# Attention scores on Trainium2: three 32-partition passes recast as one 64-partition and one 32-partition pass, with two buffers of stacked queries

## The chip, the cores and the metric

The kernel runs on one core of one Trainium2 chip. The metric is device time in microseconds (us): 2056.73 us, the median of 3 runs (2056.43 to 2056.93).

## What is computed

Two rounds of the same two layers run on x, 2048 rows of 448 floats, with the same weights in both rounds:

```python
def _A_ref(x, wq, wk, wv, wo):          # S=2048, D=448, H=16 heads, Dh=28
    q = (x @ wq).reshape(B, S, H, Dh).transpose(0, 2, 1, 3)
    k = x @ wk                          # one key and one value head for all 16
    v = x @ wv
    p = softmax(einsum("bhqd,bkd->bhqk", q, k) * (Dh ** -0.5))
    o = einsum("bhqk,bkd->bhqd", p, v)
    return o.transpose(0, 2, 1, 3).reshape(B, S, H * Dh) @ wo

def _B_ref(x, w_gate, w_up, w_down):    # F=1792
    return (silu(x @ w_gate) * (x @ w_up)) @ w_down

x = x + _A_ref(layernorm(x), ...); x = x + _B_ref(layernorm(x), ...)   # twice
```

## The kernel before, in words

**Number parts.** TensorE (PE) multiplies in a rounded 32-bit format (fp32r). Nearly all operands are therefore kept as a high part (the rounded value) and a low part (what is left), made by `split` (L131 to L133): one GpSimd (POOL) copy and one POOL subtraction. A product of two such operands is taken as three: high by high, low by high, high by low.

**Stages.** For each of the two layers: projections of queries, keys and values (`Attention.project`, `q`), then the scores, the softmax and its product with the values (`Attention.scores`), then the feed-forward layer (`FeedForward`). All engines run the program in the written order (a manual schedule).

**A group and a step.** The 2048 queries are cut into 4 chunks of 512 columns (`c`), the 16 heads into 4 sets of 4 heads (`g`). A group `i` is one pair (c, g): 16 groups in each layer. A step `n` of a group (`step`, L553) treats one tile of 128 keys (`kt`, 16 of them) against 4 heads by 512 queries, so that there are 256 steps in a layer and 512 in the program. Head `j` of the group has its 28 numbers, and 4 more rows for the bound that is subtracted ahead of the exponential, on partitions 32j to 32j+31 of the stacked queries `qts[i % 3]`. Plane 0 of that tile is the high part and plane 1 the low part. `keys[kt // 4]` repeats the same keys on all four blocks of 32 partitions, again with a high and a low plane.

**What PE does in a step.** L558 to L564 issue three passes of four matmuls; each matmul uses the 32 rows of the array of its own head, and the four of a pass use four different row groups. Heads 0 to 2 accumulate in one of two PSUM tiles of three banks (`three`), head 3 in a single bank (`one`). ScalarE (ACT) then takes the exponential of `one` (L567) and of `three` (L568). After the scores of step n, PE does `pv` (L598) of step n - 2: the exponentials as moving operand, with the tile of values as 32 weight columns, so that four heads write four blocks of 32 output partitions. That product is in full f32 and takes two instructions a head in the trace. On PE the order is: scores n, pv n - 2, scores n + 1, pv n - 1, and so on. At step 10 of groups 4, 8 and 12 the output product of the chunk before (`outproj`, L545) comes between the two.

**What feeds it.** `stack` (L371) loads the four heads of group i + 2 from DRAM (`qd`) into `qraw` with four DMAs at step 4 of group i; `parts` (L378) splits them on POOL at step 7; `rows` (L382) puts the bound's rows into partitions 28 to 31 of each block with one DMA at step 9, all DMAs on the queue of SyncE (SP). The first three groups are prepared in the projection stage, where `key_load` and `key_split` (L351, L355) also make the keys, one chunk after another. In the same stage POOL computes `rstd` (L217, L218) of the layer norm, which VectorE (DVE) needs for the normalised rows `xn` (L225), which PE transposes (L242).

`post` (L606) finishes a group: DVE copies the sums, four DMAs bring the denominators, and at step 3 of the next group `rest` sends their reciprocals through DRAM, multiplies and splits on POOL. `weights(fc)` for the feed-forward layer is called at step 8 of groups 11 to 13.

The second run of `forward` with `full=True`, under an If in the outer function, is a fallback that the shown runs do not enter; it shares the functions of the change.

Of the kernel before, what the change touches and what calls it, by code (L numbers as in the profile page):

```python
# [8 lines left out]
F32 = mybir.dt.float32  # L9
F32R = mybir.dt.float32r  # L10
# [5 lines left out]
P = 128  # L16
S = 2048
D = 448
# [8 lines left out]
FG = 2  # L27
SCALE = DH ** -0.5

LEAD = 4  # L30
LIMIT = 2.0**40
TURN = (3, 2, 0, 1)

# [20 lines left out]
def forward(  # L54
# [241 lines left out]

    GR = [(c, g) for c in range(NC) for g in range(NG)]

    class Attention:


        def __init__(self, layer):
            self.layer = layer
            self.X, self.norms, self.qd = {}, {}, {}
            self.done = 0
            self.order = [(c, m) for c in range(NC) for m in TURN]
            self.seen = 0
            self.steps, self.places = [], []
            self.lent, self.plan = None, {}
            self.hi, self.rowsof, self.kt, self.when = {}, {}, {}, {}  # L310
# [12 lines left out]
            for i in range(len(GR) if full else 0):  # L323
                fs, place = self.max_steps(i)
                if i == 1:
                    fs[KC] = lambda f=fs[KC]: (f(), self.places[0]())
                self.steps += fs
                self.places.append(place)

# [40 lines left out]

        def stack(self, i):  # L371

            c, g = GR[i]
            for j in range(4):
                r = 112 * g + DH * j
                nc.sync.dma_start(qraw[32 * j : 32 * j + DH, :], self.qd[c][r : r + DH, :])

        def parts(self, i):  # L378
            q = qts[i % 3]
            split(q[:, 0, :], q[:, 1, :], qraw)  # L380

        def rows(self, i):  # L382

            c, g = GR[i]
            src = self.rowsof[c][32 * g : 32 * g + 32, :].rearrange("n (j w) -> j n w", w=32)
            dst = qts[i % 3][28:125:32, :, :].rearrange("j z (b w) -> j (z b) w", w=32)
            nc.sync.dma_start(dst.bitcast(F32), src)

        def maxima(self, c, cands=ALL):

# [18 lines left out]
        def fetch(self, ms):  # L409

            r = wpool.tile([P, 2, 512], F32R, tag="wgl", name="wrq", bufs=FG + 1).bitcast(F32)
            two = wpool.tile([P, 2, 512], F32R, tag="wgh", name="q2", bufs=FG + 1)
            for z, m in enumerate(ms):
                nc.sync.dma_start(r[0:112, z, :], self.qd[0][112 * m : 112 * m + 112, :])
                self.hi[m] = two[0:112, z, :]
            nc.gpsimd.tensor_copy(two[0:112], r[0:112])

        def max_steps(self, i):

            got = {}  # L420
            q = qts[i % 3]

            def one(j, qt, kc):
                if not got:
                    got["mx"] = pers.tile([P, 16, KC], F32, name="mx", bufs=2)
                n = 4 * j + qt
                pm = self.mbank()[1]
                js, qs = slice(32 * j, 32 * j + 32), slice(P * qt, P * qt + P)
                for n_, (z, k) in enumerate(((0, 0), (1, 0), (0, 1))):
                    nc.tensor.matmul(  # L430
                        pm, q[js, z, qs], keys[kc][js, k, :], start=(n_ == 0), stop=(n_ == 2), tile_position=(32 * j, 0)
                    )
                nc.vector.tensor_reduce(got["mx"][:, n, kc : kc + 1], pm, AX.X, ALU.max)

            def fin():
                got["ng"] = pers.tile([P, 16], F32, name="ng", bufs=2)
                nc.vector.tensor_reduce(got["ng"], got["mx"], AX.X, ALU.max, negate=True)

            def place(pn=None):

                if pn is None:
                    pn = self.mbank()[1]
                nc.tensor.transpose(pn[0:16, 0:P], got["ng"], ident)
                nh = pers.tile([16, P], F32R, name="nh", bufs=2)
# [3 lines left out]
                for z, n_ in enumerate((nh, nl)):  # L448
                    dma(q[28:125:32, z, :].rearrange("j (t w) -> j t w", w=P), n_)
# [27 lines left out]
        def q(self, c, m):  # L477
# [6 lines left out]
                self.maxima(self.seen // 4 - 1)  # L484
            live.remove(held)
            if c not in self.qd:
                self.qd[c] = dram.tile([D, 512], F32, name=f"qd{self.layer}_{c}")
# [7 lines left out]
            nc.sync.dma_start(self.qd[c][112 * m : 112 * m + 112, :], raw[0:112, :])  # L495
# [12 lines left out]
        def finish(self):  # L508

            if self.layer:  # L510
                nc.scalar.activation(warm, halfn[:, 0:1], AF.Exp)
                if not full:
                    self.fetch((3, 2))
                    self.fetch((0, 1))
            while self.seen < len(self.order):
                self.project()
            if not full:
                self.maxima(NC - 1, (6,))
            for n in sorted(self.when):
                for f in self.when[n]:  # L520
                    f()
            self.advance(len(self.steps), NM + KC * LEAD)

        def scores(self, ff):
            next(switch)
            with tc.tile_pool(name=f"at{self.layer}", bufs=1) as wp:
                woh = wp.tile([P, NG, D], F32R, name="woh")
                wol = wp.tile([P, NG, D], F32R, name="wol")
# [24 lines left out]
                def step(n):  # L553

                    i, kt = divmod(n, NT)
                    three, one = threes[n % 2], banks[7]
                    q, k, ks = qts[i % 3], keys[kt // 4], slice(P * (kt % 4), P * (kt % 4) + P)
                    for z, (kp, part) in enumerate(((0, 0), (1, 0), (0, 1))):  # L558
                        for j in range(4):
                            js = slice(32 * j, 32 * j + 32)  # L560
                            nc.tensor.matmul(  # L561
                                three[:, j, :] if j < 3 else one, k[js, kp, ks], q[js, part, :],
                                start=(z == 0), stop=(z == 2), tile_position=(32 * j, 0),
                            )  # L564
                    pt = wp.tile([P, 3, 512], F32, name="pt", bufs=3)
                    pt1 = wp.tile([P, 512], F32, name="pt1", bufs=2 if full else 3)
# [4 lines left out]
                def between_steps(n):  # L571
# [2 lines left out]
                    free, one = threes[(n + 1) % 2], banks[7]  # L574
                    if full:
                        self.lent = free[:, 0, :]
                        self.advance(KC)
# [321 lines left out]
    at.turned(0)  # L899
    nc.gpsimd.memset(vsb, 0.0)  # L900
    nc.gpsimd.memset(vsb[:, :, DH : DH + 1], 1.0)
    nc.gpsimd.memset(qraw, 0.0)
    if mask is not None:
        nc.gpsimd.memset(mask, 0.0)
        nc.gpsimd.memset(mask[:, 0:16:5, :], 1.0)
# [47 lines left out]
```

## Time and profile before

| | |
|---|---|
| median of 3 runs | 2056.73 us |
| the profiled execution's own time | 2054.69 us |
| its span | 2053.0 us |
| PE, PE weight loads (PEld) | 2014.4 us, 1274.7 us busy |
| ACT | 1312.2 us busy |
| POOL, DVE | 535.4 us, 461.2 us busy |
| projections of layer 0 | until about 72 us |
| scores and softmax of layer 0 | about 72 to 597 us |
| feed-forward of layer 0, then the projections of layer 1 | about 597 to 1086 us |
| scores and softmax of layer 1 | about 1086 to 1609 us |
| granted TensorE clock, mean | 0.995 |

A line of a timeline gives the start in us from the start of the span, the duration in us, the engine, the line of the kernel, the operation, output and inputs with their shapes, and a count where equal neighbours are merged. A matmul's duration includes its latency, and neighbours overlap, so the distance from start to start says what it costs in a row of matmuls. "32\*128" is the shape of the array tile that is used: 32 rows (contraction) by 128 columns. In brackets stands the idle time of the engine ahead of the instruction and what is inferred to have ended it.

### The profile page before, as it was taken

The numbers are of one execution on the slowest core, as the hardware profiler recorded it, in microseconds if no ns is written. First come the engines' busy times: TensorE is split into PE (matmuls) and PEld (weight loads), VectorE is DVE, ScalarE is ACT, GpSimd is POOL, SyncE is SP. The second block draws the span as 40 slices with busy tenths as digits, with TensorE's granted clock in tenths as the row PEclk, the third lists the DMA queues.
The fourth block names the chain that finished last, engine by engine and source line by source line (L and its number), as shares of the span: only waits on it lengthen the run. The fifth ranks groups of instructions, "written<-read, shape, count | busy, mean of one in ns | idle before, by whom it ended". The sixth has DMA issues, their size and how long they took to land.

```text
span 2053.0 us, 43566 instructions
## 1 busy us (share of the span) xinstructions
PE 2014.4 (98%) x18577; PEld 1274.7 (62%) x18577; DVE 461.2 (22%) x892; ACT 1312.2 (64%) x2152; POOL 535.4 (26%) x599
## 2 busy tenths in 40 slices
PE   7999999999999999999999999999999999999997
PEld 6433434334358999999874334343343689988887
DVE  7200101001105232322451001010011242232322
ACT  4699798997964333333348998979979533333332
POOL 4213121021311333333341222101122123233320
PEclk9999999999999999999999999999999999999999
DMA  5101000011100111100031110000110000111101
GB/s 158 52 22 28 21 12 22 12 36 27 32 12 19 31 31 30 31 23 19 21 93 34 30 30 12 22 12 22 27 50 8 29 16 16 30 31 31 30 1 74
DMA packets 76516, 63.47 MB, mean 31 GB/s; under 512 B 22904, under 2 KB 63224, under 8 KB 76312
## 3 DMA queue, kind: packets, MB, share of 16 engines
q1 hardware_dynamic: 76040, 60.56, 10.4%
q8 instruction: 147, 2.41, 0.5%
q14 instruction: 57, 0.47, 0.1%
q10 hardware_dynamic: 272, 0.03, 0.0%
HBM read 47.72 MB, written 12.32 MB: 29 GB/s over the span
## 4 chain that ended last, share of the span: by engine, by line
PE 48%; ACT 46%; issue 1%; DVE 1%; DMA 0%; POOL 0%; POOLq 0%; ACTq 0%; DVEq 0%
PE bank L288 38%; ACT pt L568 31%; ACT pt L567 15%; PE bank L268 3%; PE three L545 2%; PE bank L545 2%; PE bank L242 1%; PE bank L598 1%; PE three L561 0%; PE bank L561 0%; DVE xres L732 0%; DVE sg L818 0%; DVE h L822 0%; DVE xn L225 0%; DVE xl L249 0%
## 5 line engine op out<-in xcount | busy, mean ns | idle before, releaser
L568 ACT ACTIVATE pt<-three 128x1536 f32<-128x1536 f32 x512 | 741.1, 1447 | 0.0
L598 PE MATMUL bank<-pt,vsb 128*32 128x512 f32 x4096 | 547.0, 607 | 0.6 <-ACT pt L568 0.6
L561 PEld LDWEIGHTS three<-qstack,keys 32*128 32x128 f32 x4608 | 253.6, 184 | 447.6 <-ACT pt L567 394.1
L561 PE MATMUL three<-qstack,keys 32*128 32x512 f32 x4608 | 500.8, 427 | 0.2 <-ACT pt L568 0.2
L561 PE MATMUL bank<-qstack,keys 32*128 32x512 f32 x1536 | 494.8, 427 | 4.1 <-ACT pt L567 4.1
L288 PE MATMUL bank<-xh,wgh 64*128 64x512 f32 x1728 | 452.3, 390 | 0.4
L288 PE MATMUL bank<-xh,wgl 64*128 64x512 f32 x1404 | 371.4, 390 | 0.0
L567 ACT ACTIVATE pt<-bank 128x512 f32<-128x512 f32 x512 | 305.9, 598 | 77.2 <-PE bank L561 70.7
L288 PE MATMUL bank<-xl,wgh 64*128 64x512 f32 x1296 | 338.6, 390 | 0.0
L288 PE MATMUL bank<-wdh,h 64*128 64x448 f32 x1792 | 334.2, 364 | 1.4 <-ACT h L819 0.8
L288 PEld LDWEIGHTS bank<-xh,wgh 64*128 64x128 f32 x1728 | 268.1, 184 | 17.6 <-DVE xl L249 1.5
L736 POOL TENSOR_TENSOR xres<-stage,xres 128x448 f32<-128x448 f32 x108 | 127.3, 1199 | 499.6 <-ACT stage L735 499.6
L288 PEld LDWEIGHTS bank<-wdh,h 64*128 64x128 f32 x1792 | 247.2, 184 | 15.4 <-issue 2.7
L632 POOL TENSOR_TENSOR o<-o 128x512 f32<-128x512 f32 x32 | 41.0, 1282 | 825.4 <-DMA o<-rd 748.7
L561 PEld LDWEIGHTS bank<-qstack,keys 32*128 32x128 f32 x1536 | 244.9, 184 | 5.8 <-ACT pt L567 5.5
L295 ACT COPY seen<-bank 128x1 f32<-128x1 f32 x664 | 81.9, 163 | 247.9 <-PE bank L288 245.2
L288 PEld LDWEIGHTS bank<-xh,wgl 64*128 64x128 f32 x1404 | 220.6, 184 | 12.5
L288 PE MATMUL bank<-wdl,h 64*128 64x448 f32 x896 | 220.7, 367 | 0.0
L817 ACT ACTIVATE sg<-bank 128x512 f32<-128x512 f32 x112 | 67.3, 601 | 220.1 <-PE bank L288 215.0
L288 PEld LDWEIGHTS bank<-xl,wgh 64*128 64x128 f32 x1296 | 200.3, 184 | 9.3
L598 PEld LDWEIGHTS bank<-pt,vsb 128*32 128x32 f32 x4096 | 80.9, 108 | 191.0 <-issue 176.2
L818 DVE TENSOR_TENSOR sg<-bank,sg 128x512 f32<-128x512 f32 x112 | 77.5, 692 | 501.1 <-ACT sg L817 492.1
(113 smaller groups left out, 1724.8 us busy)
## 6 DMA issues: line engine op xcount, KB each, us to landing
o<-rd SPq DMA_DIRECT2D x32, 256.0 KB
qd<-stage SPq DMA_DIRECT2D x32, 224.0 KB
qraw<-qd SPq DMA_DIRECT2D x128, 56.0 KB
wdr<-in_B_w_down_dram SPq DMA_DIRECT2D x28, 224.0 KB
wr<-in_B_w_gate_dram SPq DMA_DIRECT2D x28, 192.0 KB
wr<-in_B_w_up_dram SPq DMA_DIRECT2D x28, 192.0 KB
out_dram<-xres SPq DMA_DIRECT2D x16, 224.0 KB
xres<-in_A_x_dram SPq DMA_DIRECT2D x3, 896.0 KB
```

The lines of the kernel that those rows point to most:

```text
L268: nc.tensor.matmul(po, a, b, start=(i == 0), stop=(i == len(seq) - 1))
L288: nc.tensor.matmul(po, a, b, start=start, stop=stop, skip_group_check=True)
L295: nc.scalar.copy(seen[:, i : i + 1], po[:, 0:1])
L545: nc.tensor.matmul(po[:, 0:D], a[:, g, ts_], b[:, g, :], start=(g + z == 0), stop=(g == NG - 1 and z == 2))
L561: nc.tensor.matmul(three[:, j, :] if j < 3 else one, k[js, kp, ks], q[js, part, :], start=(z == 0), stop=(z == 2), tile_position=(32 * j, 0),)
L567: nc.scalar.activation(pt1, one, AF.Exp, scale=SCALE)
L568: nc.scalar.activation(pt, three, AF.Exp, scale=SCALE)
L598: nc.tensor.matmul(accs[i][32 * j : 32 * j + 32, :], vsb[:, kt, :], pts[n][j], start=(kt == 0), stop=(kt == NT - 1), skip_group_check=True,)
L632: nc.gpsimd.tensor_tensor(rb, oraw, rb, ALU.mult)
L736: nc.gpsimd.tensor_tensor(r, s, r, ALU.add)
L817: nc.scalar.activation(sg, pg[0], AF.Silu)
L818: nc.vector.tensor_tensor(sg, pg[1], sg, ALU.mult)
```

## The change

The three products of a head are regrouped. On the blocks of 64 partitions 0 to 63 and 64 to 127, plane 0 of the keys now holds the high part of the keys in the lower 32 partitions and their low part in the upper 32; plane 1 holds the high part everywhere. The stacked queries have three planes: planes 0 and 1 hold the high part of heads 0 and 1, and of heads 2 and 3, each head twice in a block of 64 partitions; plane 2 holds the low part of all four heads on 32 partitions each, as before. A step then does four matmuls of 64 rows (heads 0 and 1 beside each other, then heads 2 and 3), and four of 32 rows.

`parts` makes the high part of the doubled tile with one POOL copy of 1024 elements a partition, and the low part from `qraw` with a `split`; `key_split` gets two more POOL copies of 32 partitions. `stack` issues five DMAs and loads 32 rows a head instead of 28, each of four heads twice; `rows` issues three. `qd` gets 128 rows a group instead of 112. There are two buffers of stacked queries instead of three: group i + 1's `parts` are now at step 2 of group i and its `rows` at step 5, and `stack` of group i + 2 at step 9. Only two groups are prepared in the projection stage. The doubled tile lives in a buffer of the feed-forward weights, whose calls move to groups 12 to 14.

```diff
+    qts = [pers.tile([P, 3, 512], F32R, name=f"qstack{n}") for n in range(2)]
-    qts = [pers.tile([P, 2, 512], F32R, name=f"qstack{n}") for n in range(3)]
...
+    def passes(j):
+
+        r = 64 * (j % 2)
+        return (0, slice(r, r + 64), j // 2), (1, slice(32 * j, 32 * j + 32), 2)
...
-            for i in range(3):
+            for i in range(2):
                 self.at(4 + 3 * i, lambda i=i: self.stack(i))
                 self.at(6 + 3 * i, lambda i=i: self.parts(i))
...
         def key_split(self, c):
-            split(keys[c][:, 0, :], keys[c][:, 1, :], self.rep)
+            both, high = keys[c][:, 0, :], keys[c][:, 1, :]
+            split(high, both, self.rep)
+            for r in (0, 64):
+                nc.gpsimd.tensor_copy(both[r : r + 32, :], high[r : r + 32, :])
...
         def stack(self, i):
             c, g = GR[i]
+            src = self.qd[c][P * g : P * g + P, :]
+            if self.twice is None or not self.scoring:
+                self.twice = wpool.tile([P, 2, 512], F32R, tag="wgl", name="qr2", bufs=FG + 1).bitcast(F32)
             for j in range(4):
-                r = 112 * g + DH * j
-                nc.sync.dma_start(qraw[32 * j : 32 * j + DH, :], self.qd[c][r : r + DH, :])
+                head = src[DH * j : DH * j + 32, :][None].to_broadcast([2, 32, 512])
+                nc.sync.dma_start(self.twice[64 * (j % 2) : 64 * (j % 2) + 64, j // 2, :], head)
+            heads = bass.AP(tensor=src.tensor, offset=src.offset, ap=[[DH * 512, 4], [512, 32], [1, 512]])
+            nc.sync.dma_start(qraw, heads)
 
         def parts(self, i):
-            q = qts[i % 3]
-            split(q[:, 0, :], q[:, 1, :], qraw)
+            q = qts[i % 2]
+            nc.gpsimd.tensor_scalar(q[:, 0:2, :], self.twice, 1.0, 0.0, ALU.mult, ALU.add)
+            split(q[:, 2, :], q[:, 2, :], qraw)
...
         def rows(self, i):
...
+            for rs, js, dst in (
+                (slice(0, 16), slice(0, 64), q[28:93:64, 0, :]),
+                (slice(0, 16), slice(64, 128), q[28:93:64, 1, :]),
+                (slice(16, 32), slice(0, 128), q[28:125:32, 2, :]),
+            ):
+                rows = src[rs, js].rearrange("n (j w) -> j n w", w=32)
+                nc.sync.dma_start(dst.bitcast(F32).rearrange("j (n w) -> j n w", w=32), rows)
...
-                    for z, (kp, part) in enumerate(((0, 0), (1, 0), (0, 1))):
+                    for n_ in range(2):
                         for j in range(4):
-                            js = slice(32 * j, 32 * j + 32)
+                            kp, js, part = passes(j)[n_]
                             nc.tensor.matmul(
                                 three[:, j, :] if j < 3 else one, k[js, kp, ks], q[js, part, :],
-                                start=(z == 0), stop=(z == 2), tile_position=(32 * j, 0),
+                                start=(n_ == 0), stop=(n_ == 1), tile_position=(js.start, 0),
                             )
...
-                    if kt == 4 and 2 < i + 2 < len(GR):
+                    if kt == (0 if full else 2) and 1 < i + 1 < len(GR):
+                        self.parts(i + 1)
+                    if kt == 5 and 1 < i + 1 < len(GR) and not full:
+                        self.rows(i + 1)
+                    if kt == 9 and i + 2 < len(GR):
                         self.stack(i + 2)
-                    if kt == 7 and 2 < i + 2 < len(GR):
-                        self.parts(i + 2)
-                    if kt == 9 and 2 < i + 2 < len(GR) and not full:
-                        self.rows(i + 2)
...
-                    if kt == 8 and 10 < i <= 11 + FG:
-                        ff.W[i - 11] = weights(i - 11)
+                    if kt == 8 and 11 < i <= 12 + FG:
+                        ff.W[i - 12] = weights(i - 12)
```

More of the change, by code (lines that the diff above doesn't have):

```diff
@@ L28 @@
 SCALE = DH ** -0.5
-LEAD = 4
 LIMIT = 2.0**40
@@ L309, in __init__ @@
             self.lent, self.plan = None, {}
+            self.twice, self.scoring = None, False
             self.hi, self.rowsof, self.kt, self.when = {}, {}, {}, {}
@@ L373, in stack @@
             c, g = GR[i]
+            src = self.qd[c][P * g : P * g + P, :]
+            if self.twice is None or not self.scoring:
+                self.twice = wpool.tile([P, 2, 512], F32R, tag="wgl", name="qr2", bufs=FG + 1).bitcast(F32)
             for j in range(4):
-                r = 112 * g + DH * j
-                nc.sync.dma_start(qraw[32 * j : 32 * j + DH, :], self.qd[c][r : r + DH, :])
+                head = src[DH * j : DH * j + 32, :][None].to_broadcast([2, 32, 512])
+                nc.sync.dma_start(self.twice[64 * (j % 2) : 64 * (j % 2) + 64, j // 2, :], head)
+            heads = bass.AP(tensor=src.tensor, offset=src.offset, ap=[[DH * 512, 4], [512, 32], [1, 512]])
+            nc.sync.dma_start(qraw, heads)
         def parts(self, i):
-            q = qts[i % 3]
-            split(q[:, 0, :], q[:, 1, :], qraw)
+            q = qts[i % 2]
+            nc.gpsimd.tensor_scalar(q[:, 0:2, :], self.twice, 1.0, 0.0, ALU.mult, ALU.add)
+            split(q[:, 2, :], q[:, 2, :], qraw)
+            if full:
+                for dst in (q[28:93:64, 0, :], q[28:93:64, 1, :], q[28:125:32, 2, :]):
+                    dma(dst, self.kt[0][29:30, :].to_broadcast([dst.shape[0], 512]))
         def rows(self, i):
             c, g = GR[i]
-            src = self.rowsof[c][32 * g : 32 * g + 32, :].rearrange("n (j w) -> j n w", w=32)
-            dst = qts[i % 3][28:125:32, :, :].rearrange("j z (b w) -> j (z b) w", w=32)
-            nc.sync.dma_start(dst.bitcast(F32), src)
+            src, q = self.rowsof[c][32 * g : 32 * g + 32, :], qts[i % 2]
+            for rs, js, dst in (
[5 more added lines that the diff above has]
+                nc.sync.dma_start(dst.bitcast(F32).rearrange("j (n w) -> j n w", w=32), rows)
         def maxima(self, c, cands=ALL):
@@ L420, in max_steps @@
             got = {}
-            q = qts[i % 3]
+            q = qts[i % 2]
             def one(j, qt, kc):
@@ L427, in one @@
                 pm = self.mbank()[1]
-                js, qs = slice(32 * j, 32 * j + 32), slice(P * qt, P * qt + P)
-                for n_, (z, k) in enumerate(((0, 0), (1, 0), (0, 1))):
+                qs = slice(P * qt, P * qt + P)
+                for n_, (k, js, z) in enumerate(passes(j)):
                     nc.tensor.matmul(
-                        pm, q[js, z, qs], keys[kc][js, k, :], start=(n_ == 0), stop=(n_ == 2), tile_position=(32 * j, 0)
+                        pm, q[js, z, qs], keys[kc][js, k, :], start=(n_ == 0), stop=(n_ == 1),
+                        tile_position=(js.start, 0),
                     )
@@ L447, in place @@
                 nc.vector.tensor_tensor(nl, pn[0:16, 0:P], nh, ALU.subtract)
-                for z, n_ in enumerate((nh, nl)):
-                    dma(q[28:125:32, z, :].rearrange("j (t w) -> j t w", w=P), n_)
+                for dst, n_ in (
+                    (q[28:93:64, 0, :], nh[0:8]), (q[28:93:64, 1, :], nh[8:16]), (q[28:125:32, 2, :], nl)
+                ):
+                    dma(dst.rearrange("j (t w) -> j t w", w=P), n_)
             order = [(j, qt, kc) for j in range(4) for qt in range(4) for kc in range(KC)]
@@ L486, in q @@
             if c not in self.qd:
-                self.qd[c] = dram.tile([D, 512], F32, name=f"qd{self.layer}_{c}")
+                self.qd[c] = dram.tile([NG * P, 512], F32, name=f"qd{self.layer}_{c}")
             raw = self.pool.tile([P, 512], F32, name="stage")
@@ L521, in finish @@
                     f()
-            self.advance(len(self.steps), NM + KC * LEAD)
+            if full:
+                self.advance(NM)
+                self.places[0]()
         def scores(self, ff):
             next(switch)
+            self.twice, self.scoring = None, True
             with tc.tile_pool(name=f"at{self.layer}", bufs=1) as wp:
@@ L576, in between_steps @@
                         self.lent = free[:, 0, :]
-                        self.advance(KC)
+                        self.advance(6, min(NM * (i + 2), len(self.steps)))
                         if kt == 11 and i + 1 < len(GR):
@@ L901, in forward @@
     nc.gpsimd.memset(vsb[:, :, DH : DH + 1], 1.0)
-    nc.gpsimd.memset(qraw, 0.0)
     if mask is not None:
```

8 lines of the change are left out of this document (3 added, 5 removed).

## The prediction, on record before the result was known

> **What bounds the kernel now.** I read the page first (busy time, then the shares of the chain of waits), then one stretch of the scores by windows, and then two steps of it in the timeline.
>
> ```profile
> PE 2014.4 (98%) x18577; PEld 1274.7 (62%) x18577; DVE 461.2 (22%) x892; ACT 1312.2 (64%) x2152; POOL 535.4 (26%) x599
> PE 48%; ACT 46%; issue 1%; DVE 1%; DMA 0%; POOL 0%; POOLq 0%; ACTq 0%; DVEq 0%
> L568 ACT ACTIVATE pt<-three 128x1536 f32<-128x1536 f32 x512 | 741.1, 1447 | 0.0
> L567 ACT ACTIVATE pt<-bank 128x512 f32<-128x512 f32 x512 | 305.9, 598 | 77.2 <-PE bank L561 70.7 <-DMA qd<-stage 2.7 <-issue 2.7
> 363.00:482.00 119.00, 119.00 (x1256) 41.16 (x1252) 6.22 (x24) 118.96 (x125) 22.76 (x22) 1.00 0.13 30
> ```
>
> The third line counts 512 steps, one large exponential each; the fourth has the small ones, with 77.2 us of idle time ahead of them in the whole span. In the 119 us of the last line, all scores, PE is busy for 119.00 us and ACT for 118.96 us, so busy time cannot say which of them sets the step. The chain gives 46% to ACT, which reads as "the scores are bound by ACT". I do not take that over, because of these lines:
>
> ```profile
> 401.18 0.51 PE L561 MATMUL three<-qstack,keys 32*128 32x512 f32 x3
> 401.28 0.19 PEld L561 LDWEIGHTS three<-qstack,keys 32*128 32x128 f32 x3
> 401.51 0.41 PE L561 MATMUL three<-qstack,keys 32*128 32x512 f32 x3
> 401.74 0.41 PE L561 MATMUL three<-qstack,keys 32*128 32x512 f32 x3
> 402.08 0.16 PEld L598 LDWEIGHTS bank<-pt,vsb 128*32 128x32 f32 x8 [0.37 <-issue]
> 402.26 0.60 ACT L567 ACTIVATE pt<-bank 128x512 f32<-128x512 f32 x1
> 403.08 0.19 PEld L561 LDWEIGHTS three<-qstack,keys 32*128 32x128 f32 x3 [0.84 <-ACT pt L567]
> 404.17 0.60 ACT L567 ACTIVATE pt<-bank 128x512 f32<-128x512 f32 x1
> ```
>
> ```profile
> 596.52 0.16 PEld L598 LDWEIGHTS bank<-pt,vsb 128*32 128x32 f32 x8 [1.18 <-ACT pt L568]
> 597.52 0.19 PEld L268 LDWEIGHTS bank<-xh,wgh 128*128 128x128 f32 x1 [0.84 <-issue]
> 233.15 0.60 ACT L567 ACTIVATE pt<-bank 128x512 f32<-128x512 f32 x1 [0.23 <-ACT pt L568]
> 234.97 0.60 ACT L567 ACTIVATE pt<-bank 128x512 f32<-128x512 f32 x1
> 402.21 0.04 issue
> ```
>
> A step lasts 403.08 - 401.18 = 1.90 us on PE: 0.90 us from the first load of the scores to the first load of pv (402.08), and 1.00 us from there to the next scores. The bracket at 403.08 names ACT, but that exponential began at 402.26 and ended at 402.86, 0.22 us before. The next two lines settle it: after the last pv, PE goes on with a projection that waits for no exponential, and its first load also comes 597.52 - 596.52 = 1.00 us after pv's. So PE is never kept waiting in a normal step; pv takes that long. ACT has room: after a hiccup it does a step in 234.97 - 233.15 = 1.82 us, and in the steady state the chain has 0.04 us a step in which it does nothing (last line). **PE sets the step, with ACT 0.08 us behind it.** What the change costs PE in a step is paid in full 512 times; what it saves is paid back for 0.08 us at most.
>
> **The change part by part: the rounds.** The second and third passes start 0.23 us apart (401.51, 401.74), and the second starts 0.23 us after its own weights began to load (401.28), since loads are made behind the running pass. So a round of four matmuls on 32 rows costs 0.22 to 0.23 us. After the change, heads 0 and 1 stream beside each other on 64 rows, then heads 2 and 3 through the same rows, and then all four on 32 rows: again three rounds. The nearest rows for a round of 64 rows are the feed-forward pairs:
>
> ```profile
> 1008.75 0.39 PE L268 MATMUL bank<-xh,wh 128*128 128x512 f32 x1
> 1008.97 0.39 PE L268 MATMUL bank<-xh,wl 128*128 128x512 f32 x1
> 1009.29 0.19 PEld L288 LDWEIGHTS bank<-xh,wgh 64*128 64x128 f32 x2 [0.35 <-issue]
> 1009.40 0.19 PEld L288 LDWEIGHTS bank<-xl,wgh 64*128 64x128 f32 x2
> 1009.63 0.39 PE L288 MATMUL bank<-xl,wgh 64*128 64x512 f32 x2
> 1009.86 0.40 PE L288 MATMUL bank<-xh,wgl 64*128 64x512 f32 x2
> ```
>
> Two pairs start 0.23 us apart. Three rounds for three rounds: nothing saved by streaming, although the matmuls fall from 12 to 8.
>
> **The switch between the rounds.** New is that the array goes from 64-row tiles to 32-row tiles inside each step. No row of before shows that switch. The lines above show the nearest, from 128 to 64 rows: the last matmul of the old shape starts at 1008.97, the first load of the new one at 1009.29 (0.32 us later, instead of behind the old matmul), and the second load at 1009.40, which is when the first pair starts to stream. Start to start that is 0.43 us instead of 0.22 to 0.23: a switch costs 0.20 us, about half of it a drain and half (0.11 us) a load that is no longer hidden. The other direction, with 448 columns:
>
> ```profile
> 1003.56 0.37 PE L288 MATMUL bank<-wdl,h 64*128 64x448 f32 x2
> 1003.77 0.36 PE L288 MATMUL bank<-wdh,h 64*128 64x448 f32 x2
> 1004.06 0.19 PEld L268 LDWEIGHTS bank<-xh,wh 128*128 128x128 f32 x1 [0.31 <-issue]
> 1004.17 0.19 PEld L268 LDWEIGHTS bank<-xl,wh 128*128 128x128 f32 x1
> ```
>
> Here 0.40 us stand in place of 0.21: 0.19 us. The bounds of the unknown switch are 0 (row groups that don't mind each other; a gain by the switch itself is excluded, as it adds no stream and removes none) and 0.26 us (the reading plus half a load, for four tiles to load instead of two). I take 0.205 us, from the 512-column rows, which are the same width as the scores. The switch from pv into the scores and the one from the 32-row round into pv are there already and stay. So the step becomes 1.90 + 0.205 = 2.105 us, above ACT's 1.82, and the sum for PE is 512 x 0.205 = **105 us**.
>
> The Trainium skill speaks against the change here: "TensorEngine Tiling (Array Packing)", Key Properties, says that a change of the tiling mode, unlike a change of tile within one mode, drains TensorE, and lists 64 and 32 rows as different modes. The rows between 128 and 64 agree (0.19 and 0.20 us); no run yet shows 64 to 32. By that rule the sum stays at 105 us, without it there would be no term.
>
> **Group buffers.** With two buffers, `parts` of group i + 1 waits until the scores of group i - 1 are done, which they are at step 0, two steps earlier than it is issued. Its price on POOL and that of the DMAs:
>
> ```profile
> L132 POOL TENSOR_SCALAR qstack<-qraw 128x512 fp32r<-128x512 f32 x32 | 19.9, 620 | 0.2
> L133 POOL TENSOR_TENSOR qstack<-qraw,qstack 128x512 fp32r<-128x512 f32 x32 | 41.1, 1286 | 2.7
> L132 POOL TENSOR_SCALAR wgh<-wr 128x1024 fp32r<-128x1024 f32 x28 | 29.3, 1048 | 0.2 <-DMA wr<-in_B_w_up_dram 0.2
> 208.17 1.77 SPq L376 DMA_DIRECT2D qraw<-qd  x4
> 1234.72 0.57 SPq L387 DMA_DIRECT2D qstack<-rows  x1
> ```
>
> POOL: 1.05 + 0.62 + 1.29 = 2.96 us instead of 1.91, from step 2 to before step 4. Behind it in the queue is `rest` of step 3, whose data come through DRAM later still. SP: five stack DMAs at 0.44 us (1.77 / 4) and three of 0.57 us for the rows, 3.9 us a group of some 30 us. Behind `rows` on SP (waiting for `parts`) stands only the stack of step 9. The rows leave by step 7 at the latest and are needed at step 16, about 17 us later: hidden, cost nothing. If that cover were gone, each late microsecond would count 30 times. The weights one group later are still 24 steps ahead of the end of the layer.
>
> **The projections.** `key_split` gets two copies of 512 elements a partition, about 0.62 us each by the row above (an estimate; 32 partitions instead of 128). In layer 0 one place feels it:
>
> ```profile
> 45.95 1.29 POOL L133 TENSOR_TENSOR keys<-wrk,keys 128x512 fp32r<-128x512 f32 x1
> 47.33 0.20 POOL L217 TENSOR_SCALAR rstd<-mv 128x4 f32<-128x4 f32 x1
> 48.66 1.78 DVE L225 TENSOR_SCALAR xn<-xres,mv,rstd 128x448 f32<-128x448 f32 x4 [1.72 <-POOL rstd L218]
> 50.27 1.47 PE L242 MATMUL bank<-ident,xn 128*128 128x128 f32 x12
> ```
>
> `rstd` follows the key split at once, DVE waits for it, and PE transposes as soon as `xn` is there. So 1.3 us more on POOL arrive on PE: +1.3 us. The same split in layer 1 has no such follower. The third group's preparation falls away there, but it lay beside PE's work: nothing. Between nothing and twice that, 0 to 2.6 us.
>
> **Sum.** 2054.69 + 105.0 + 1.3 = 2161.0 us for an execution like the profiled one (span 2053.0 and 1.7 us around it). The median of the runs was 2.0 us above that execution, so I predict 2163 us for the median, 5.2% slower.
>
> **The rivals.** (a) *The switch is free*: row groups are independent, the 32-row loads slip behind the last 64-row round. Then the change does to the time only the 1.3 us: 2058 us. For it: within one shape, loads do run behind the matmuls of the same rows. Against: from 128 to 64 rows they don't, though only row groups differ there too. (b) *Faster*: the switch is free, and fewer instructions count. The place is the two rounds that become pairs; the price is the difference of a round to the 0.22 us that I read as the best spacing, 0.01 us each, so 0.02 x 512 = 10 us: 2058 - 10 = 2048 us. It decides only if a switch costs under 0.02 us. Against: pairs (1009.63 to 1009.86) are no closer together than fours. (c) *Only the drain is paid*: the 32-row weights are loaded while the 64-row round streams, and 0.10 us a step is left: 2058 + 51 = 2109 us. Against: in both switches above the load itself waits for the drain. (d) *The stacked queries come late* at the group boundaries, as they have one spare buffer less: with 1.5 us at each of 30 boundaries, on top of the forecast, 2208 us. It decides only from a delay of some 17 us.
>
> For (c) the Trainium skill has a rule: "TensorE: Matmul & The Clock Gate", the table at its head, says that the engine's queue is a partial reorder window that pulls weight loads ahead of matmuls in flight. The loads at 401.28 agree, the load at 1009.29 does not: it came only after the drain.
>
> **How the numbers follow.** Forecast 0.80; (a) 0.07; (b) 0.03; (c) 0.06; (d) 0.04. Within the forecast the switch may be 0.15 us (drain and half a load) to the bound of 0.26 us, so 2058 + 77 = 2135 to 2058 + 133 = 2191 us. The four rivals lie outside and hold 0.20, so this is the range. About 0.2% (4 us) is what a measurement of this kernel can tell from no change. Faster by more than that: (b), 0.03. Within: (a), 0.07. Slower: forecast, (c) and (d), 0.90.
>
> **What would show it.** In the scores' timeline: two starts of 64-row matmuls 0.23 us apart, then a 32-row load 0.32 us after the second, its matmuls 0.11 us later, and pv's first load 1.10 us after the step's first load instead of 0.90. The large exponentials should start 2.10 us apart, and ACT should show about 0.2 us of idle time a step in front of L567, put down to PE: some 110 us in all in place of the 77.2. Right for the buffers would be no wait of PE on POOL or DMA at the first step of a group; right for layer 0, scores that begin about 1.3 us later. If the 32-row loads stand beside 64-row matmuls and the step stays at 1.90 us, the forecast has failed at the switch; if steps are 2.10 us but the time is above 2191 us, look at the group boundaries.

## The result, and the profile after

The changed kernel takes 2182.28 us (median of 4 runs, 2181.69 to 2182.9) beside 2056.58 us for the kernel before on the same chip: ratio 1.0613, 95% interval 1.06 to 1.0625. The forecast of 2163 us lay 19 us below; the measured time is inside its range of 2135 to 2191 us. The profiled execution took 2182.05 us with a span of 2180.0 us, against 2053.0 us before.

From the page of the changed kernel, the busy times, the shares of the chain of waits, and the group of the small exponentials (busy us, mean ns, idle us ahead of them and what ended it):

```profile
PE 2119.3 (97%) x16529; PEld 1269.2 (58%) x16529; DVE 460.9 (21%) x892; ACT 1332.3 (61%) x2152; POOL 578.1 (27%) x646
PE 92%; DMA 3%; ACT 1%; DVE 1%; SPq 1%; POOL 1%; issue 0%; POOLq 0%; ACTq 0%; DVEq 0%
L596 ACT ACTIVATE pt<-bank 128x512 f32<-128x512 f32 x512 | 306.2, 598 | 154.8 <-PE bank L590 143.4
```

2048 matmuls fewer (16529 in place of 18577), and PE is busy 105 us longer. The chain, which had put 46% on ACT, now has 92% on PE and 3% on DMA. ACT's idle time ahead of L596 has doubled, from 77.2 to 154.8 us, and nearly all of it waits for the scores.

One step of the scores in the timeline of the changed kernel:

```profile
401.94 0.29 PEld L590 LDWEIGHTS three<-qstack,keys 64*128 64x128 f32 x3 [0.84 <-ACT pt L596]
402.28 0.39 PE L590 MATMUL bank<-qstack,keys 64*128 64x512 f32 x1
402.60 0.19 PEld L590 LDWEIGHTS three<-qstack,keys 32*128 32x128 f32 x3 [0.36 <-issue]
403.04 0.16 PEld L627 LDWEIGHTS bank<-pt,vsb 128*32 128x32 f32 x8 [0.25 <-issue]
403.22 0.60 ACT L596 ACTIVATE pt<-bank 128x512 f32<-128x512 f32 x1 [0.15 <-PE bank L590]
404.03 0.29 PEld L590 LDWEIGHTS three<-qstack,keys 64*128 64x128 f32 x3 [0.84 <-ACT pt L596]
```

The step is 404.03 - 401.94 = 2.09 us in place of 1.90. From its first load to pv's it is 1.10 us in place of 0.90; from there to the next step 0.99 us, as before. The line to look at is the third: the loads of the 32-row round come 0.32 us after the last 64-row matmul began, not behind it. Where before all loads of the scores in a step but the first were hidden, one more now stands bare.

The limits of the stages, from the first load of the scores and the first load of the feed-forward layer, in both layers, in the timeline of the changed kernel:

```profile
81.24 0.29 PEld L590 LDWEIGHTS three<-qstack,keys 64*128 64x128 f32 x3 [0.24 <-issue]
656.47 0.19 PEld L267 LDWEIGHTS bank<-xh,wgh 128*128 128x128 f32 x1 [0.84 <-issue]
1163.51 0.31 PEld L590 LDWEIGHTS three<-qstack,keys 64*128 64x128 f32 x3 [0.28 <-issue]
1738.37 0.19 PEld L267 LDWEIGHTS bank<-xh,wgh 128*128 128x128 f32 x1 [0.84 <-issue]
```

and the same four in the kernel before (the second of them stands in the prediction):

```profile
71.21 0.19 PEld L561 LDWEIGHTS three<-qstack,keys 32*128 32x128 f32 x3 [0.24 <-issue]
...
1085.97 0.19 PEld L561 LDWEIGHTS three<-qstack,keys 32*128 32x128 f32 x3 [0.24 <-issue]
1611.93 0.19 PEld L268 LDWEIGHTS bank<-xh,wgh 128*128 128x128 f32 x1 [0.84 <-issue]
```

| stage, us | before | after | difference |
|---|---|---|---|
| start to scores of layer 0 | 71.2 | 81.2 | +10.0 |
| scores of layer 0 | 526.3 | 575.2 | +48.9 |
| feed-forward of layer 0, projections of layer 1 | 488.4 | 507.0 | +18.6 |
| scores of layer 1 | 526.0 | 574.9 | +48.9 |

These are 126.4 of the 127.0 us. The scores' share is 97.8 us, 0.191 us for each of 512 steps. The other 28.6 us are lost ahead of the scores, in the projections, where the prediction had 1.3 us. There the DMA queue's timeline and POOL's show this (layer 0):

```profile
32.43 4.22 SPq L387 DMA_DIRECT2D qr<-qd  x4
36.69 2.52 SPq L389 DMA_DIRECT2D qraw<-qd  x1
```

```profile
48.18 1.06 POOL L394 TENSOR_SCALAR qstack<-qr 128x1024 fp32r<-128x1024 f32 x1 [8.54 <-DMA qr<-qd]
50.74 0.63 POOL L131 TENSOR_SCALAR qstack<-qraw 128x512 fp32r<-128x512 f32 x1 [1.49 <-DMA qraw<-qd]
53.87 0.62 POOL L131 TENSOR_SCALAR keys<-wrk 128x512 fp32r<-128x512 f32 x1
57.24 0.20 POOL L216 TENSOR_SCALAR rstd<-mv 128x4 f32<-128x4 f32 x1
```

The doubled load leaves at 32.43 us and is there at 48.1; POOL, which works in order, stands before `parts`, and the keys and `rstd` behind it come 8.6 and 9.9 us later than before (45.25 and 47.33). What the DMA engines do meanwhile, by windows (start and end, length, the busy time of PE, PEld, DVE, ACT and POOL, and as the last three numbers the granted TensorE clock, the share of the 16 DMA engines and GB/s):

```profile
46.00:48.00 2.00, 2.00 (x10) 1.67 (x9) 0.91 (x4) 0.00 (x0) 0.00 (x0) 1.00 0.13 50
48.00:50.00 2.00, 1.78 (x8) 1.13 (x6) 0.00 (x0) 0.00 (x0) 1.06 (x1) 1.00 0.13 49
50.00:52.00 2.00, 0.00 (x0) 0.00 (x0) 0.00 (x0) 0.50 (x2) 1.18 (x2) 0.93 0.13 49
54.00:56.00 2.00, 0.28 (x1) 0.00 (x0) 0.00 (x0) 0.04 (x1) 1.85 (x3) 0.50 0.26 71
```

A share that stays at 0.13 is what two engines of sixteen give (the trace doesn't name the engine of a packet). PE runs dry at 50 us, and after that the granted clock is 0.50, so that the work after the gap is slower too: matmuls of 512 columns then start 0.43 us apart (64.93 to 65.36), not 0.23. The kernel before has such a gap there as well, but a short one: 2.55 us of waiting ahead of 54.30 us, and its matmuls are 0.23 us apart again by 58.3. In layer 1 the same jam reaches PE by another way, in the list of waits of the whole run:

```profile
POOL qstack L394 <- DMA qr<-qd: 54.5, 8, 8.8
ACT stage L520 <- DMA kt<-stage: 29.0, 4, 14.8
PE bank L241 <- DVE vt L527: 20.6, 5, 15.0
```

(total us, times, longest). The longest waits of the last two lines lie in layer 1: SP issues the small `kt<-stage` transfers only behind the doubled loads (at 1134.57 and 1136.37 us, the loads at 1126.96), and one lands late (whether it stands in the queues of the same two engines is not shown); ACT cannot reuse its `stage` buffer until 1144.52, DVE waits for ACT, and PE for DVE until 1146.06, for 15 us.

### The profile page after: what moved, and what is told of

Same layout as the page of the kernel before. It is cut to its first block, busy times and chain, and to the rows that moved or that the text cites. A ratio compares the mean times of both kernels' runs of the same rounds, so it can differ in the third digit from the quotient of the medians.

```text
span 2180.0 us, 39731 instructions
## 1 busy us (share of the span) xinstructions
PE 2119.3 (97%) x16529; PEld 1269.2 (58%) x16529; DVE 460.9 (21%) x892; ACT 1332.3 (61%) x2152; POOL 578.1 (27%) x646
## 4 chain that ended last, share of the span: by engine, by line
PE 92%; DMA 3%; ACT 1%; DVE 1%; SPq 1%; POOL 1%; issue 0%; POOLq 0%; ACTq 0%; DVEq 0%
PE bank L287 36%; PE three L590 26%; PE bank L627 23%; PE bank L267 3%; PE three L574 2%; DMA qraw<-qd 2%; PE bank L574 2%; PE bank L241 1%; DMA kt<-stage 1%; SPq L387 0%; DMA wrk<-kt 0%; ACT pt L597 0%; ACT pt L596 0%; DMA qd<-stage 0%; PE bank L590 0%
## 5 line engine op out<-in xcount | busy, mean ns | idle before, releaser
L590 PEld LDWEIGHTS three<-qstack,keys 64*128 64x128 f32 (+1 forms) x3072 | 248.5, 183 | 618.0 <-ACT pt L596 390.7
L590 PE MATMUL three<-qstack,keys 64*128 64x512 f32 (+1 forms) x3072 | 600.1, 480 | 0.8 <-ACT pt L597 0.7
L590 PE MATMUL bank<-qstack,keys 64*128 64x512 f32 (+1 forms) x1024 | 424.3, 444 | 3.7 <-ACT pt L596 3.7
L596 ACT ACTIVATE pt<-bank 128x512 f32<-128x512 f32 x512 | 306.2, 598 | 154.8 <-PE bank L590 143.4
L590 PEld LDWEIGHTS bank<-qstack,keys 64*128 64x128 f32 (+1 forms) x1024 | 189.3, 185 | 4.5 <-ACT pt L596 4.5
L640 DVE COPY o<-bank 128x512 f32<-128x512 f32 x32 | 22.1, 692 | 751.5 <-PE bank L627 751.5
```

The source lines that it names most:

```text
L590: nc.tensor.matmul(three[:, j, :] if j < 3 else one, k[js, kp, ks], q[js, part, :], start=(n_ == 0), stop=(n_ == 1), tile_position=(js.sta ...
L596: nc.scalar.activation(pt1, one, AF.Exp, scale=SCALE)
```

## The experiments

Theory: two causes that add up, the change of the array's shape in each step (98 us), and the doubled loads that go through two DMA engines (about 20 us of the 28). Rivals are named with each run. Medians and ratios stand against the kernel before on the same chip (2056.6 to 2057.7 us); step times are the length of both layers' scores divided by 512. In e2, e4, e5 and e7 to e10 the If around the fallback also tests `ok == 1` in place of `ok == 0`, so that other sums do not lead into the fallback; the diffs below leave that line out.

| run | median us | ratio (95%) | step, us | scores of layer 0 begin | feed-forward and projections |
|---|---|---|---|---|---|
| before | 2056.6 | 1 | 2.055 | 71.2 | 488.4 |
| after | 2182.3 | 1.0613 (1.06 to 1.0625) | 2.246 | 81.2 | 507.0 |
| e3 one more switch | 2276.9 | 1.1078 (1.1059 to 1.1096) | 2.432 | 80.9 | 507.0 |
| e2 three 32-row rounds | 2089.1 | 1.016 (1.0142 to 1.0177) | 2.065 | 81.0 | 507.4 |
| e4 four 64-row rounds | 2196.5 | 1.068 (1.0662 to 1.0697) | 2.275 | 79.9 | 508.8 |
| e5 two rounds, before | 2020.1 | 0.9829 (0.9812 to 0.9845) | 1.984 | 71.4 | 490.2 |
| e1 spread loads | 2161.0 | 1.0498 (1.0481 to 1.0516) | 2.245 | 78.7 | 491.2 |
| e6 spread copies only | 2166.7 | 1.0534 (1.0516 to 1.0551) | 2.243 | 77.8 | 495.3 |
| e9 leading two | 2181.2 | 1.0605 (1.0587 to 1.0623) | 2.246 | 81.0 | 506.8 |
| e10 flat 64 rows | 2161.4 | 1.0505 (1.0487 to 1.0523) | 2.243 | 76.5 | 492.6 |
| e7 no key copies | 2157.0 | 1.0491 (1.0474 to 1.0509) | 2.243 | 73.1 | 492.1 |
| e8 spread, three rounds | 2061.6 | 1.0025 (1.0015 to 1.0035) | 2.056 | 73.7 | 491.3 |

(The mean step holds the output products of the chunks too, so that it is 0.15 us above a single step.)

### The switch in the step

**e3**: the same eight matmuls, the 32-row round between the two 64-row rounds.

```diff
-                    for n_ in range(2):
-                        for j in range(4):
-                            kp, js, part = passes(j)[n_]
+                    for j, n_ in ((0, 0), (1, 0), (0, 1), (1, 1), (2, 1), (3, 1), (2, 0), (3, 0)):
+                        kp, js, part = passes(j)[n_]
+                        first = n_ == (j > 1)
...
-                                start=(n_ == 0), stop=(n_ == 1), tile_position=(js.start, 0),
+                            start=first, stop=not first, tile_position=(js.start, 0),
```

> The changed kernel with the same eight matmuls in another order: heads 0 and 1 on 64 rows, then all four on 32 rows, then heads 2 and 3 on 64 rows. The number of rounds is the same, the array changes its shape once more in a step. Switch theory: 0.19 to 0.205 us more a step, 97 to 105 us, so 2279 to 2288 us. Rival, that 64-row rounds are just longer than 32-row rounds beside a 32-row round and no price hangs on the change of shape: within 10 us of 2182 us.

Measured: 2276.85 us, 94.6 us more than the change, a little under the stated span; its mean step is 2.432 - 2.246 = 0.186 us longer, the price of the added switch. A step of e3 in the timeline of the weight loads:

```profile
432.09 0.19 PEld L590 LDWEIGHTS three<-qstack,keys 64*128 64x128 f32 x2 [0.84 <-ACT pt L596]
432.52 0.19 PEld L590 LDWEIGHTS three<-qstack,keys 32*128 32x128 f32 x3 [0.24 <-issue]
432.95 0.18 PEld L590 LDWEIGHTS three<-qstack,keys 64*128 64x128 f32 x1 [0.24 <-issue]
433.38 0.16 PEld L627 LDWEIGHTS bank<-pt,vsb 128*32 128x32 f32 x8 [0.24 <-issue]
434.37 0.19 PEld L590 LDWEIGHTS three<-qstack,keys 64*128 64x128 f32 x2 [0.84 <-ACT pt L596]
```

Each round now stands alone: 0.43 us from load to load, in either direction, in place of 0.22 to 0.23 us where the shape stays. Same matmuls, same data: the price hangs on the change of shape.

**e2**: the change with three rounds of 32 rows (only the high keys are used, so the scores are other sums).

```diff
-                    for n_ in range(2):
+                    for n_ in range(3):
                         for j in range(4):
-                            kp, js, part = passes(j)[n_]
+                            js = slice(32 * j, 32 * j + 32)
...
-                                three[:, j, :] if j < 3 else one, k[js, kp, ks], q[js, part, :],
+                                three[:, j, :] if j < 3 else one, k[js, 1, ks], q[js, n_, :],
```

> The changed kernel, but with three rounds of four 32-row matmuls in a step, as before the change; all its loads, copies, buffers and places stay. The scores are then sums of other products than the reference's (only the high keys are used). Switch theory: the step goes back to 1.90 us, 98 us go, and the time is 2056.6 + 28 = 2085 us (2082 to 2088). Rival, that the later order of the loads and two buffers lengthen the steps: steps stay above 1.95 us and the time above 2110 us.

Measured: 2089.12 us, 1 us above the stated span; the mean step falls to 2.065 us. What is left against before is 31.5 us: 28.8 in the projections, which are as in the changed kernel (81.0 and 507.4 us), and some 3 to 5 us in the scores. Most of these lie at the first output product of each layer, where pv comes 13.39 and 14.97 us after the pv before it, and in e8, which has e2's rounds but other loads, 12.09 and 12.28: so they seem to hang on the loads, not on the steps.

**e4**: no change of shape between the rounds, but four of them (high keys by high queries again in place of the queries' low parts).

```diff
-                            kp, js, part = passes(j)[n_]
+                            js = passes(j)[0][1]
...
-                                three[:, j, :] if j < 3 else one, k[js, kp, ks], q[js, part, :],
+                                three[:, j, :] if j < 3 else one, k[js, n_, ks], q[js, j // 2, :],
```

> The changed kernel with the second pass also on 64 rows: four rounds of two 64-row matmuls in a step, and no change of shape between them. The scores then contain other products than the reference's (high by high on the second pass instead of the low parts of the queries). Switch theory: a round more costs 0.23 us, the missing switch gives 0.19 to 0.205 back beyond one round's own cost, so a step of 1.90 + 0.225 = 2.12 us against 2.095 us: 2182 + 13 to 16 = 2195 to 2200 us. Rival, that 64-row rounds are slower than 32-row rounds in themselves (0.29 us each would explain the 0.19): four of them give 1.90 + 0.225 + 4 x 0.06 = 2.37 us, about 2320 us.

Measured: 2196.53 us, as the switch theory has it. Two 64-row rounds in place of the 32-row round and its switch cost 0.029 us a step more than the change, 0.220 us more than before. So a 64-row round costs what a 32-row round costs, and the rival that they are slower in themselves is out.

**e5**: the kernel before without its third pass.

```diff
-                    for z, (kp, part) in enumerate(((0, 0), (1, 0), (0, 1))):
+                    for z, (kp, part) in enumerate(((0, 0), (1, 0))):
...
-                                start=(z == 0), stop=(z == 2), tile_position=(32 * j, 0),
+                                start=(z == 0), stop=(z == 1), tile_position=(32 * j, 0),
```

> The kernel before, with the third pass of the scores left out (the low parts of the queries aren't used, so the scores are less exact). It shows what is behind PE in a step. Theory: PE would need 1.90 - 0.225 = 1.675 us, ACT 1.82 us, so ACT sets the step and 0.08 us a step are gained, 41 us: 2015 us (2010 to 2022). Rival, that ACT already sets the step, as the chain of waits reads: 2057 us, within 6 us.

Measured: 2020.05 us, 36.6 us less than before. Two small exponentials in a row in its timeline, and the large one between them:

```profile
419.86 0.96 ACT L567 ACTIVATE pt<-bank 128x512 f32<-128x512 f32 x1
420.36 1.82 ACT L568 ACTIVATE pt<-three 128x1536 f32<-128x1536 f32 x1
421.69 0.96 ACT L567 ACTIVATE pt<-bank 128x512 f32<-128x512 f32 x1
```

The step is 1.83 us. PE lost 0.225 us of work (the prediction's reading of a round) and the step only 0.07: that is where ACT takes over, just behind PE, at the 1.82 us that the prediction had read for it. The large exponential, which begins at 420.36 and lasts 1.82 us, is not over when the next small one begins at 421.69; the recorded durations overlap (in the kernel before the two last 1.45 and 0.60 us). The rival, that ACT had set the step before, is out: then nothing would have been won. This is the only run below the kernel before, and it gives up the products with the queries' low parts.

### The loads in the projections

**e1** and **e6**: the same rows by other DMAs; e6 has the first hunk alone.

```diff
             for j in range(4):
-                head = src[DH * j : DH * j + 32, :][None].to_broadcast([2, 32, 512])
-                nc.sync.dma_start(self.twice[64 * (j % 2) : 64 * (j % 2) + 64, j // 2, :], head)
+                for r in (64 * (j % 2), 64 * (j % 2) + 32):
+                    nc.sync.dma_start(self.twice[r : r + 32, j // 2, :], src[DH * j : DH * j + 32, :])
...
-            heads = bass.AP(tensor=src.tensor, offset=src.offset, ap=[[DH * 512, 4], [512, 32], [1, 512]])
-            nc.sync.dma_start(qraw, heads)
+            for j in range(4):
+                nc.sync.dma_start(qraw[32 * j : 32 * j + 32, :], src[DH * j : DH * j + 32, :])
```

> The changed kernel with the same bytes loaded by other DMAs: each copy of a head, and each head of qraw, gets a DMA of 32 rows of its own (12 instead of 5), with no broadcast over two copies. Theory A: of the 126 us, 98 are the switch inside the steps and 28 are the projections, where the broadcast DMAs land 14 us after their issue because their packets go through few DMA engines at a time; POOL and the later small DMAs stand behind them. Then the loads land within 6 us, layer 0's scores begin at about 73 us instead of 81, the second layer's gap shrinks by some 16 us, and the time is 2155 to 2162 us. Theory B: it is the amount of data (768 KB instead of 224 KB a group) and the work of issuing; then twelve DMAs are no better than five and the time is 2180 us or more.

> As e1, but only the doubled copies are loaded by eight DMAs of 32 rows; qraw keeps its one DMA over four heads. Theory A (few engines for the two-fold broadcast, 256 packets): nearly all of e1's gain, 2156 to 2166 us. If the single DMA of qraw is the slow one: within 5 us of the changed kernel, 2177 to 2183 us.

Measured: 2161.0 us (2156.95 to 2163.23) and 2166.7 us, 21 and 16 us under the change, e6 just above its span. With twelve DMAs SP issues more of them, and yet the time falls, so neither the bytes nor the issuing is the cause. The stretch between the layers shrinks by 15.8 us. One part missed: layer 0's scores begin at 78.7 us in e1, not at about 73; but that execution was 2.8 us late before any of the changed loads (first `rstd` at 35.01 us, before: 32.22), and e8, with the same loads, begins at 73.7.

**e9** and **e10** ask what makes the loads slow. Both keep four DMAs of 64 partitions and the bytes; the doubled tile then holds other rows, so the scores are other sums. e9 first, then e10:

```diff
-                head = src[DH * j : DH * j + 32, :][None].to_broadcast([2, 32, 512])
+                two = src[32 * (j % 2) : 32 * (j % 2) + 32, :]
+                head = bass.AP(tensor=two.tensor, offset=two.offset, ap=[[DH * 512, 2], [512, 32], [1, 512]])
...
-                head = src[DH * j : DH * j + 32, :][None].to_broadcast([2, 32, 512])
+                head = src[64 * (j % 2) : 64 * (j % 2) + 64, :]
```

> The changed kernel; each of its four copy DMAs again moves two blocks of 32 rows into 64 partitions, but from two different places (28 rows apart) instead of the same place twice. The doubled tile then holds other rows than it should, and the scores are other sums than the reference's. If the slow landing comes from the shape of the transfer (a leading count of two, each block through one of the 16 DMA engines): as slow as the changed kernel, 2178 to 2186 us. If it comes from reading the same DRAM rows twice (the broadcast): as fast as with spread copies, 2160 to 2170 us.

> The changed kernel; each of its four copy DMAs reads 64 rows that lie one after another, so that the transfer has one leading count of 64; same number of DMAs, same bytes, same place in the queue. The doubled tile holds other rows than it should, and the scores are other sums than the reference's. If the leading count sets over how many engines the packets go: as with spread copies, 2158 to 2168 us, and no stretch with a DMA share of 0.13 for long. If it is the size of a single DMA, or 768 KB in all: 2178 to 2186 us.

Measured: 2181.15 us and 2161.37 us. Two different blocks are as slow as the same block twice; one block of 64 rows in order is as fast as spread copies. (It is 5 us faster than e6, which loads `qraw` in the same way; why is not shown.) The same windows in e9 and in e10:

```profile
48.00:50.00 2.00, 2.00 (x10) 1.67 (x9) 1.40 (x5) 0.00 (x0) 0.99 (x1) 1.00 0.13 50
50.00:52.00 2.00, 2.00 (x10) 1.52 (x9) 0.00 (x0) 0.00 (x0) 0.51 (x2) 1.00 0.13 49
```

```profile
48.00:50.00 2.00, 2.00 (x10) 1.66 (x9) 1.56 (x5) 0.64 (x2) 1.85 (x3) 1.00 0.73 218
50.00:52.00 2.00, 2.00 (x10) 1.68 (x9) 0.00 (x0) 0.82 (x2) 1.78 (x4) 1.00 0.51 135
```

So it is neither the broadcast nor the size: with a leading count of two in the transfer's pattern, its 128 KB move at the pace of two engines. e9's source also lies in two pieces and e10's in one, but pieces alone do not slow a load: with the weight loads, most of them 384 rows of 512 bytes that lie apart with a leading count of 128, the DMA share is 0.66 and 0.70 (kernel before, 674 to 676 us). The Trainium skill has the rule, in "DMA: Bandwidth & Descriptors", Rules for kernel authors: an outermost dimension of c below 16, a zero-stride broadcast for one, confines a DMA to at most c engines. The share of 0.13 and e9 agree with it.

### What is left

**e7**: e1 without the two POOL copies of the keys (the scores then lack the products of two high parts).

```diff
             split(high, both, self.rep)
-            for r in (0, 64):
-                nc.gpsimd.tensor_copy(both[r : r + 32, :], high[r : r + 32, :])
```

> The kernel with spread loads (e1), without the two POOL copies in the split of the keys (plane 0 of the keys then holds low parts only, so the scores lack the high by high products). In e1's trace 5 us of the projections are left beside the kernel before. If the copies carry what the prediction said: 1.3 us less than e1, by way of rstd in layer 0; at most 3 us. If the rest is the longer parts and the loads: no difference to e1 within 1 us of the two profiles' starts of the scores.

Measured: 2157.0 us, 4 us under e1, more than either guess, though e1's own runs spread over 6 us. Nearly all of the difference lies ahead of layer 0's scores (73.1 us); between the layers there is none (492.1 and 491.2). But part of it is e1's late start. From the first `rstd` (35.01 us in e1, 32.81 in e7) to the first scores e1 takes 43.7 us and e7 40.2; e8 (below), which has e1's loads and the copies, takes 41.6 (32.13 to 73.72). So the place was as predicted; by these single executions the price is between 1.3 us, as predicted, and 3.5 us, and not settled better.

**e8**: e1's loads and e2's rounds in one kernel.

> e1 and e2 together: the changed kernel with spread loads and three rounds of 32-row matmuls; the scores again use the high keys only. If the two causes add up and nothing else is hidden in the change: 2057.6 + 126 - 98 - 21 = 2063 us (2058 to 2067). If two buffers or the later parts cost something of their own that the switch had covered: above 2070 us.

Measured: 2061.6 us, 0.25% above before. The scores take 526.3 and 526.6 us, before 526.3 and 526.0: two buffers, three DMAs for the rows and the longer `parts` cost the steps nothing. The 5 us that are left lie in the projections: 2.5 us ahead of layer 0's scores and 2.9 us between the layers. No run shows what the latter are; it is not the key copies, as e7, which leaves them out, loses as much there (492.1).

## Why the prediction was right, and where it was not

- **PE sets the step, ACT is 0.08 us behind.** Right: e5 finds ACT 0.07 us a step behind PE. The bracket and the chain that named ACT were misleading, and the pair of loads 1.00 us apart with no exponential between them was the better witness.
- **Three rounds for three rounds, nothing saved by streaming.** Right: 0.23 us a round of 64 rows (402.05 to 402.28 us in the changed kernel), and e4's four rounds cost one round more.
- **The switch, 0.205 us, 105 us in all.** Right in mechanism, 7% too large: 0.191 us a step by the stages, 98 us and 0.186 us for e3's. The drain was read well (0.32 us to the load), and the Trainium skill's rule on tiling modes ("TensorEngine Tiling (Array Packing)", Key Properties) holds between 64 and 32 rows too. The rivals (a), (b) and (c) are out.
- **Group buffers cost nothing.** Right, by e8; rival (d) is out. The doubled loads land late in the scores too (POOL waits 8.79 us for one ahead of `parts` at 188.37 us), but there the cover hides it.
- **The projections, +1.3 us.** Wrong in size, and the only step that failed: 28.6 us. The prediction priced the doubled loads by what SP needs to issue them (0.44 us each), a price taken from loads of 28 rows in order, and put their landing at nothing: the 17 us of slack that it names are those of the bound's rows in the scores. In the projections the slack is a few microseconds: before, `parts` began 6 us after its loads left. About 21 us (medians of e1 and e10) to 23 us (the stages of e8) come from the landing at the pace of two engines, some 5 us from the rest (e8), of which the key copies are 1.3 to 3.5.
- **The range** holds the time partly by luck: its upper end was drawn for a dearer switch (0.26 us, 28 us above the forecast), and that room took up the 27 us missing in the projections, less the 7 us by which the switch had been put too high. The two errors went opposite ways.
- **The sign of ACT's idle time** was as said, the amount not: 154.8 us where "some 110" was named; 0.15 to 0.17 us of each step, instead of 0.2, but on top of the old 77.

## What to carry to other kernels

Count array shapes, not matmuls: with tiled matmuls, a pass of fewer instructions that needs another tile shape in the same step pays a drain and a bare weight load, here 0.19 us each time. When a load is doubled, look at the order of its access pattern before its bytes: with an outermost count of two it went at the pace of two DMA engines, and engines that work in order, here POOL, pass the delay on to everything behind it. And when two engines look equally busy, take out some work of one: what the step gains tells how far the other is behind.

## What the runs showed of the hardware that was not expected

- A transfer of 64 rows of 2 KB with a leading count of two ran at 49 to 50 GB/s with a DMA share of 0.13, and ACT waited up to 14.8 us for a `kt<-stage` of 24 or 32 KB issued behind such loads; the same bytes with a leading count of 64 let the stretch reach 218 GB/s.
- Issuing got dearer with them: in the projections the four doubled loads took SP 4.22 us, where four loads of 28 rows had taken 1.71 us (31.96 us in the kernel before); in the scores 2.30 us (132.03) in place of 1.77.
- A switch between 64-row and 32-row tiles costs the same both ways: 0.43 us from load to load in e3, as from 128 to 64 rows in the kernel before.
